# All batches' attention weights and values multiplied as float32, without splitting, in an attention and two-layer MoE kernel

## The chip, the cores and the metric

The kernel runs on one core of a Trainium2 chip. Its time is the device time of one execution in microseconds (us). TensorE multiplies matrices, VectorE, ScalarE and GpSimd work elementwise, and SyncE issues most of the transfers. In rows of the profile they are PE (PEld for its weight loads), DVE, ACT, POOL and SP.

## The reference

```
q, k, v: 8 batches x 8 heads x 576 x 64, float32
k_p, v_p = k, v averaged over groups of 8 positions      # 72 pooled positions
attn = softmax(q @ k_p.T / 8)                            # 576 x 72 per head
x = (attn @ v_p) as 4608 tokens x 512
h = max(x @ w1, x @ w2, x @ w3)                          # 4608 x 768
x = h @ w_out                                            # 4608 x 512
h = max(x @ w_in, 0);  out = (h * h) @ moe2_w_out        # 512 -> 2048 -> 512
```

## The kernel before

The 4608 tokens are worked on in 12 blocks of 384 for attention and the first layer, and then in 9 blocks of 512 for the second layer. A batch has 576 tokens, so it falls on the blocks in two pieces, one of 384 tokens and one of 192. A piece is worked on by pairs of heads, four pairs to a batch (`attend`): `load` brings k, q and v; `prepare` pools k into `kbd`; `softmax` multiplies (L353, into `sc`), takes the exponentials and normalises them; `transpose` turns the weights round on TensorE (L381, into `tr`) and copies them to `pt`; `values` multiplies them with the pooled values and writes `x`.

The products of the MoE layers are made exact to nearly float32 by splitting: a number is rounded to the reduced float32 type of TensorE (`fp32r` in rows), and what is lost becomes a second number of that type, so that the product is a sum of three reduced products (`PARTS`). `split` writes both halves: the high one by ScalarE (L133), the low one by VectorE or, for weights, GpSimd (L134).

Attention has two ways of forming the values, chosen by `whole = b < NATURAL`, where NATURAL is 1:

- Batch 0 (`whole`): its values are pooled by TensorE (`pool_v`). `transpose` copies the weights of one head by ScalarE (L389) and of the other by VectorE (L387), as float32. `values` makes one float32 product for each head, both into the one bank `av0` (L398), and splits the sum into `x`.
- Batches 1 to 7: VectorE pools the values (L242), and ScalarE and VectorE split them (L209, L210) into `vst`. The weights of each head are split on the way out of `tr` (L384, L385). `values` makes two reduced products for each head (L409 for the high half of the weights, L410 for the low), with the high and low values side by side in the stationary matrix, so that the two sums land in two halves of the partitions of bank `av0` or `av1`. ScalarE copies one half (L412), VectorE adds the other (L413), both through the buffer `xf`, and `xf` is split into `x`.

The transposed weights of the second head use bank `av1` too. Pieces of work are put into a list `todo` with due times and run in that order, after which a scheduler places each engine's instructions by its own timeline. In the first 115 us the weights of the first layer are converted as well (`convert`: L160 and L161 on ScalarE, L162 and L165 on VectorE; then L133 and L134 on GpSimd), on loads that share four `raw` buffers with k and v. Attention is woven into the first layer's products (L513, and L532 for its output) up to about 698 us; the second layer (L673, L797) runs from 762 us.

Of the kernel before, what the change touches and what calls it, by code (L numbers as in the profile page):

```python
# [10 lines left out]
F32 = mybir.dt.float32  # L11
F32R = mybir.dt.float32r
I32 = mybir.dt.int32
U32 = mybir.dt.uint32
AF = mybir.ActivationFunctionType
ALU = mybir.AluOpType
# [4 lines left out]
P = 128  # L21
B, H, S, D = 8, 8, 576, 64
POOL = 8
SP = S // POOL
NPAIR = H // 2
# [8 lines left out]
T1 = 384  # L34
# [35 lines left out]
NATURAL = 1  # L70
# [12 lines left out]
def as_f32(ap):  # L83
    return ap.bitcast(F32)
# [8 lines left out]
def attention_moe_kernel(ctx: ExitStack, tc: tile.TileContext, q, k, v, vn, w1, w2, w3, wo1, wi2, wo2, out):  # L93
    nc = tc.nc
# [12 lines left out]
    for sign, base in ((1, POOL * MID), (-1, POOL - 1 - POOL * MID)):  # L107
        nc.gpsimd.affine_select(
            out=sums, in_=sums, compare_op=ALU.is_ge, fill=0.0, base=base,
# [26 lines left out]
    def split(hl, src, engine=nc.vector):  # L136

        split_to(hl[:, 0], hl[:, 1], src, engine)
# [43 lines left out]
    t_p = s1.enter_context(tc.tile_pool(name="t_p", bufs=2))  # L182

    s_at = ctx.enter_context(ExitStack())
    kv_p = s_at.enter_context(tc.tile_pool(name="kv_p", bufs=1, side="right"))
    raw_p = s_at.enter_context(tc.tile_pool(name="raw_p", bufs=4, side="right"))
    sm_p = s_at.enter_context(tc.tile_pool(name="sm_p", bufs=4, side="right"))
    pt_p = s_at.enter_context(tc.tile_pool(name="pt_p", bufs=2, side="right"))
    xf_p = s_at.enter_context(tc.tile_pool(name="xf_p", bufs=1, side="right"))
    ah_p = s_at.enter_context(tc.tile_pool(name="ah_p", bufs=AHEAD, side="right"))  # L190
    sc_ps = s_at.enter_context(tc.tile_pool(name="sc_ps", bufs=2, space=PSUM))
    tr_ps = s_at.enter_context(tc.tile_pool(name="tr_ps", bufs=1, space=PSUM))
    av_ps = s_at.enter_context(tc.tile_pool(name="av_ps", bufs=1, space=PSUM))


    vst = kv_p.tile([SP, NPAIR, 4, D], F32R, name="vst")

    kbd = kv_p.tile([P, NPAIR, 2, SP], F32, name="kbd")
    nc.gpsimd.memset(kbd, 0.0)
    vst_f = []  # L200
    for _ in range(2):
        vf = t_p.tile([P, T1], F32, tag="ys", name="vst_f")[:SP].rearrange("s (p a d) -> s p a d", a=3, d=D)
        nc.gpsimd.memset(vf, 0.0)
        vst_f.append(vf)
    K_SCALE = 1.0 / (POOL * D**0.5)
    V_SCALE = 1.0 / POOL

    def split_scaled(hi, lo, src, scale):
        nc.scalar.activation(hi, src, AF.Copy, scale=scale)  # L209
        nc.vector.scalar_tensor_tensor(  # L210
            out=lo, in0=src, scalar=scale, in1=as_f32(hi), op0=ALU.mult, op1=ALU.subtract
        )


    spare = [f"spare{i}" for i in range(KF1)]
# [24 lines left out]
    def prepare_v(p, vr):  # L240
        vs = sm_p.tile([SP, 2, D], F32, tag="vs", name="vs", bufs=2)
        nc.vector.tensor_reduce(out=vs, in_=vr, axis=AX.X, op=ALU.add)  # L242
        split_scaled(vst[:, p, 0:4:3], vst[:, p, 1:3], vs, V_SCALE)

    def load_natural(b):

# [11 lines left out]
    def pool_v(tiles):  # L258
        vp = mm_ps.tile([P, 512], F32, tag="ps", name="vp")[:SP]
        last = (S - 1) // P  # L260
        for i in range(last + 1):
            n = min(P, S - i * P)
            c = MID - i * P // POOL
            nc.tensor.matmul(
                vp, lhsT=sums[:n, c : c + SP], rhs=tiles[i // 2][:n, i % 2], start=(i == 0), stop=(i == last)
            )
        for h in range(2):
            vh = vp.rearrange("s (p h d) -> s h p d", h=2, d=D)[:, h]
            for i in range(2):
                nc.scalar.activation(vst_f[i][:, :, 2 * h], vh[:, 2 * i : 2 * i + 2], AF.Copy, scale=V_SCALE)  # L270

    x_t = {}

# [45 lines left out]
    def attend(j, b, s0, n, p, t):  # L319

        kr, vr, qr, pt, sms = [], [], [], [], []
        first, whole = s0 == 0, b < NATURAL

        def load():
            if j == 0:
                kq = early([P, 2 * 512], "kq")
                kr.append(kq[:, :S])
                qr.append(kq[:, S : S + n])
                nc.sync.dma_start(out=kr[0], in_=k[b, p])
            elif first:  # L330
                kr.append(load_k(b, p))
            if j:
                qr.append(raw_p.tile([P, T1], F32, tag="qr", name="qr", bufs=4)[:, :n])
            nc.sync.dma_start(out=qr[0], in_=q[b, p, :, s0 : s0 + n])
            if first and b >= NATURAL:
                vr.append(load_v(b, p))

        def prepare():
            if first:
                prepare_k(p, kr[0])  # L340

        tiles = score_tiles(n)
        m = tiles[0][1]

        def softmax():
            if vr:
                prepare_v(p, vr.pop())
            g = len(tiles)
            sc = sc_ps.tile([P, 3 * 2 * SP], F32, tag="sc", name="sc")
            ss = scores(g)[:m]  # L350
            src = sc[:, : g * 2 * SP].rearrange("p (g h s) -> p g h s", h=2, s=SP)[:m]
            for i, (c, _) in enumerate(tiles):
                nc.tensor.matmul(src[:, i], lhsT=qr[0][:, c : c + m], rhs=kbd[:, p], start=True, stop=True)  # L353
            st = sm_p.tile([P, 3, 3, 2], F32, tag="st", name="st")[:m, :, :g]
            nc.vector.tensor_reduce(out=st[:, 0], in_=src, axis=AX.X, op=ALU.max, negate=True)  # L355
            for i in range(g):
                for h in range(2):
                    nc.scalar.activation(  # L358
                        ss[:, i, h], src[:, i, h], AF.Exp, bias=st[:, 0, i, h : h + 1],
                        accum_out=st[:, 1, i, h : h + 1],  # L360
                    )
            nc.vector.tensor_scalar_add(st[:, 1], st[:, 1], 1e-9)
            nc.vector.reciprocal(st[:, 2], st[:, 1])  # L363
            nc.gpsimd.tensor_tensor(  # L364
                out=ss, in0=ss,
                in1=st[:, 2].rearrange("p g (h o) -> p g h o", o=1).to_broadcast([m, g, 2, SP]), op=ALU.mult,
            )
            sms.append(ss)

        def transpose():  # L370
            if whole:
                pt.append(pt_p.tile([SP, 2, T1], F32, tag="pt", name="pt"))
            else:
                pt.append(pt_p.tile([SP, 2, 2, T1], F32R, tag="pt", name="pt"))
            for h in range(2):
                if h:
                    tr = av_ps.tile([P, T1], F32, tag="av1", name="tr")[:SP, :n]
                else:
                    tr = tr_ps.tile([SP, T1], F32, tag="tr", name="tr")[:, :n]
                for i, (c, _) in enumerate(tiles):  # L380
                    nc.tensor.transpose(tr[:, c : c + m], sms[0][:, i, h], ident[:m, :m])  # L381
                if not whole:
                    hi, lo = pt[0][:, 0, h, :n], pt[0][:, 1, h, :n]
                    nc.scalar.activation(hi, tr, AF.Copy)  # L384
                    nc.vector.tensor_tensor(out=lo, in0=tr, in1=as_f32(hi), op=ALU.subtract)  # L385
                elif h:
                    nc.vector.tensor_copy(pt[0][:, h, :n], tr)  # L387
                else:
                    nc.scalar.activation(pt[0][:, h, :n], tr, AF.Copy)  # L389

        def values():
            if t == 0:
                x_t[j][p] = x_p.tile([P, 2, T1], F32R, tag="x", name="x")
            x = x_t[j][p][:, :, t : t + n]
            if whole:
                av = av_ps.tile([P, T1], F32, tag="av0", name="av0")[:, :n]
                for h in range(2):
                    nc.tensor.matmul(  # L398
                        av, lhsT=vst_f[p // 2][:, p % 2, h : h + 2].rearrange("p a d -> p (a d)"), rhs=pt[0][:, h, :n],
                        start=(h == 0), stop=(h == 1),  # L400
                    )
                split(x, av)
                return
            hi, lo = pt[0][:, 0, :, :n], pt[0][:, 1, :, :n]
            xf = xf_p.tile([P, T1], F32, tag="xf", name="xf")[:, :n]
            for h in range(2):
                av = av_ps.tile([P, T1], F32, tag=f"av{h}", name=f"av{h}")[:, :n]
                lhsT = vst[:, p, 2 * h : 2 * h + 2].rearrange("p a d -> p (a d)")
                nc.tensor.matmul(av, lhsT=lhsT, rhs=hi[:, h], start=True, stop=False)  # L409
                nc.tensor.matmul(av, lhsT=lhsT, rhs=lo[:, h], start=False, stop=True)  # L410
                r, o = slice(h * D, (h + 1) * D), slice((1 - h) * D, (2 - h) * D)
                nc.scalar.activation(xf[r], av[o], AF.Copy)  # L412
                nc.vector.tensor_tensor(out=xf[r], in0=av[r], in1=xf[r], op=ALU.add)  # L413
            split(x, xf)

        return load, prepare, softmax, transpose, values

    w1_t, wo1_t = {}, {}
# [454 lines left out]
```

## Time and profile before

| | |
|---|---|
| median of three runs | 1467.43 us (1466.56 to 1469.72) |
| the profiled execution | 1465.84 us |
| its span, first to last instruction | 1464.0 us |
| TensorE busy | 1432.9 us (98%) |
| VectorE busy | 984.6 us (67%) |
| ScalarE busy | 763.9 us (52%) |
| GpSimd busy | 182.2 us (12%) |
| mean granted clock of TensorE | 0.993 |

The span leaves 1.8 us of the profiled execution's time outside. The busy time of an engine is the time in which at least one of its instructions is in flight; TensorE's instructions overlap, so that the distance between the starts of two of them, not their duration, says how long each holds up the next. A float32 product appears as two records of TensorE, a reduced product or a transpose as one.

### The profile page before, as it was taken

The page shows a single profiled execution, that of the slowest core. Times are in us where ns is not written, and L with a number is a line of the kernel's source. Part 1 is how long each engine was busy: PE and PEld are TensorE (multiplying, and loading weights), DVE is VectorE, ACT ScalarE, POOL GpSimd, SP SyncE. Part 2 cuts the span into 40 slices and gives each one's busy share as a digit, 9 for nine tenths or more (in the row PEclk, how much of TensorE's full clock was granted, in tenths as well). Part 3 has the DMA queues.
Part 4 walks back from the last instruction along what each step waited for, and adds up shares of the span by engine and source line. Part 5 has one row for each costly group of instructions (what it writes and reads, how often), then busy time and mean ns, then how long its engine had stood idle before and what let it go on. Part 6 is the DMA issues. An engine that isn't in the chain of part 4 may idle for free.

```text
span 1464.0 us, 27554 instructions
## 1 busy us (share of the span) xinstructions
PE 1432.9 (98%) x10410; PEld 1409.8 (96%) x10410; DVE 984.6 (67%) x1778; ACT 763.9 (52%) x1983; POOL 182.2 (12%) x228
## 2 busy tenths in 40 slices
PE   6989999999999999999999999999999999999998
PEld 4879999999999999999999999999999999999998
DVE  5896466766765856656426768687776768686765
ACT  7794366655665646655314535353444445454443
POOL 3451012222222212222000000000000000000000
PEclk9899999999999999999999999999999999999999
DMA  7553135443355434422539856666666666565746
GB/s 225 185 168 110 53 115 173 141 134 123 120 164 176 126 124 130 130 101 79 187 116 370 290 196 212 220 210 224 229 231 225 227 216 214 198 245 174 274 144 229
DMA packets 118307, 263.94 MB, mean 180 GB/s; under 512 B 12672, under 2 KB 62848, under 8 KB 118176
## 3 DMA queue, kind: packets, MB, share of 16 engines
q1 hardware_dynamic: 111264, 252.75, 51.0%
q10 hardware_dynamic: 6912, 9.44, 1.8%
q8 instruction: 82, 1.34, 0.4%
q14 instruction: 49, 0.40, 0.1%
HBM read 213.91 MB, written 48.23 MB: 179 GB/s over the span
## 4 chain that ended last, share of the span: by engine, by line
PE 88%; DMA 5%; ACT 3%; DVE 2%; issue 1%; POOL 0%; SPq 0%; DVEq 0%; ACTq 0%; POOLq 0%
PE ps L513 28%; PE ps L673 23%; PE ps L532 10%; PE accB L797 6%; PE accA L797 6%; DMA wo2s<-wo_dram 4%; PE accF L797 3%; PE accE L797 3%; PE sc L353 2%; PE accD L797 2%; PE tr L381 2%; PE av L410 1%; PE av L409 1%; ACT ss L358 1%; DVE wbits L165 1%
## 5 line engine op out<-in xcount | busy, mean ns | idle before, releaser
L513 PE MATMUL ps<-x,w 128*128 128x384 f32 x2592 | 495.7, 342 | 3.3 <-ACT w L133 1.2
L513 PEld LDWEIGHTS ps<-x,w 128*128 128x128 f32 x2592 | 452.0, 190 | 6.1 <-ACT w L133 2.6
L673 PE MATMUL ps<-y,wi2s 128*128 128x256 f32 x3024 | 371.8, 277 | 0.5 <-DVE c L644 0.2
L673 PEld LDWEIGHTS ps<-y,wi2s 128*128 128x128 f32 x3024 | 356.6, 188 | 1.9 <-DVE c L644 0.8
L532 PE MATMUL ps<-h,wo 128*128 128x384 f32 x864 | 162.1, 339 | 3.2 <-POOL wo L134 2.4
L532 PEld LDWEIGHTS ps<-h,wo 128*128 128x128 f32 x864 | 149.5, 189 | 4.0 <-POOL wo L134 2.8
L686 ACT ACTIVATE c<-c 128x512 f32<-128x512 f32 x90 | 56.3, 627 | 167.2 <-DVE c L644 166.6
L644 DVE TENSOR_TENSOR c<-ps,c 128x512 f32<-128x512 f32 x144 | 98.2, 687 | 66.0 <-PE ps L673 64.5
L521 DVE TENSOR_TENSOR hm<-ps,hm 128x384 f32<-128x384 f32 x144 | 79.5, 552 | 72.3 <-PE ps L513 69.9
L133 ACT ACTIVATE g<-c 128x512 fp32r<-128x512 f32 x144 | 90.2, 626 | 56.7 <-DVE c L683 23.3
L797 PE MATMUL accA<-wo2s,g 128*128 128x256 f32 x864 | 115.8, 277 | 0.0
L797 PE MATMUL accB<-wo2s,g 128*128 128x256 f32 x864 | 110.9, 277 | 2.6 <-DMA wo2s<-wo_dram 1.9
L134 DVE TENSOR_TENSOR g<-c,g 128x512 fp32r<-128x512 f32 x144 | 97.6, 685 | 16.2 <-ACT g L133 16.2
L797 PEld LDWEIGHTS accA<-wo2s,g 128*128 128x128 f32 x864 | 107.1, 188 | 0.0
L358 ACT ACTIVATE ss<-sc,st 128x72 f32<-128x72 f32 (+1 forms) x320 | 97.9, 319 | 17.6 <-DVE st L355 15.4
L797 PEld LDWEIGHTS accB<-wo2s,g 128*128 128x128 f32 x864 | 103.9, 188 | 3.2 <-ACT o L766 1.6
L364 POOL TENSOR_TENSOR ss<-ss,st 128x432 f32<-128x432 f32 (+1 forms) x64 | 56.4, 882 | 265.7 <-DVE st L363 182.9
L413 DVE TENSOR_TENSOR xf<-av,xf 64x192 f32<-64x192 f32 (+1 forms) x112 | 50.7, 453 | 46.7 <-ACT xf L412 44.8
L385 DVE TENSOR_TENSOR pt<-tr,pt 72x192 fp32r<-72x192 f32 (+1 forms) x112 | 49.3, 449 | 41.4 <-ACT pt L384 40.1
L412 ACT ACTIVATE xf<-av 64x192 f32<-64x192 f32 (+1 forms) x112 | 45.4, 405 | 54.5 <-PE av L410 40.4
L133 ACT ACTIVATE h<-hm 128x384 fp32r<-128x384 f32 x72 | 37.7, 523 | 64.2 <-DVE hm L521 63.9
L358 ACT ACTIVATION_READ_ACCUMULATOR ss<-sc,st 128x1 f32 (+1 forms) x320 | 65.8, 206 | 0.0
(104 smaller groups left out, 1951.4 us busy)
## 6 DMA issues: line engine op xcount, KB each, us to landing
wo2s<-wo_dram SPq DMA_DIRECT2D x252, 512.0 KB, 5.7
wi2s<-wi_dram SPq DMA_DIRECT2D x24, 512.0 KB, 9.1
wraw<-in_wo_dram SPq DMA_DIRECT2D x22, 512.0 KB, 3.7
wraw<-in_w_dram SPq DMA_DIRECT2D x18, 512.0 KB, 3.4
y_dram<-ys ACTq DMA_DIRECT2D x48, 192.0 KB, 2.0
wraw<-in_wi_dram SPq DMA_DIRECT2D x16, 512.0 KB, 3.5
wi_dram<-wraw SPq DMA_DIRECT2D x16, 512.0 KB, 3.7
wo_dram<-wraw SPq DMA_DIRECT2D x64, 128.0 KB, 2.0
```

The source lines that it names most:

```text
L133: nc.scalar.activation(hi, src, AF.Copy)
L134: engine.tensor_tensor(out=lo, in0=src, in1=as_f32(hi), op=ALU.subtract)
L358: nc.scalar.activation(ss[:, i, h], src[:, i, h], AF.Exp, bias=st[:, 0, i, h : h + 1], accum_out=st[:, 1, i, h : h + 1],)
L364: nc.gpsimd.tensor_tensor(out=ss, in0=ss, in1=st[:, 2].rearrange("p g (h o) -> p g h o", o=1).to_broadcast([m, g, 2, SP]), op=ALU.mult,)
L413: nc.vector.tensor_tensor(out=xf[r], in0=av[r], in1=xf[r], op=ALU.add)
L513: nc.tensor.matmul(ps, lhsT=w1_t[f, e][:, a, kk * P : (kk + 1) * P], rhs=x[kk][:, c], start=(n == 0), stop=(n == 3 * KD - 1),)
L521: nc.vector.tensor_tensor(out=hm, in0=ps, in1=hm, op=ALU.max)
L532: nc.tensor.matmul(ps, lhsT=wo1_t[kk][:, a, d * P : (d + 1) * P], rhs=hs[kk][:, c], start=(n == 0), stop=(n == 3 * KF1 - 1),)
L644: nc.vector.tensor_tensor(out=out, in0=in0, in1=in1, op=ALU.add)
L673: nc.tensor.matmul(bank[:, u * HT : (u + 1) * HT], lhsT=wi2_t[2 * gr + u][i][:, a, o + kk * P : o + (kk + 1) * P], rhs=y_t[j][m][:, c, kk] ...
L686: nc.scalar.activation(c, c, AF.Relu)
L797: nc.tensor.matmul(bank[:, i * 256 : (i + 1) * 256], lhsT=g[:, a, u * HT + i * P : u * HT + (i + 1) * P], rhs=w[:, u, c], start=(n == 0 an ...
```

## The change

Every batch is now handled as batch 0 was in `transpose` and `values`: the weights are copied once for each head, there is one float32 product for each head, and `x` is split straight from the bank. The branch for split values, the buffer `xf`, and `split_scaled` are gone; `vst` holds unsplit float32 values with a zero block between the heads, for all batches (batch 0's had buffers of their own). VectorE still pools the values of batches 1 to 7 (`prepare_v`), and ScalarE alone writes them to `vst`.

```diff
-    xf_p = s_at.enter_context(tc.tile_pool(name="xf_p", bufs=1, side="right"))
-    vst = kv_p.tile([SP, NPAIR, 4, D], F32R, name="vst")
-    vst_f = []
-    for _ in range(2):
-        vf = t_p.tile([P, T1], F32, tag="ys", name="vst_f")[:SP].rearrange("s (p a d) -> s p a d", a=3, d=D)
-        nc.gpsimd.memset(vf, 0.0)
-        vst_f.append(vf)
+    vst = kv_p.tile([SP, NPAIR, 3, D], F32, name="vst")
+    nc.gpsimd.memset(vst, 0.0)
...
-        split_scaled(vst[:, p, 0:4:3], vst[:, p, 1:3], vs, V_SCALE)
+        nc.scalar.activation(vst[:, p, 0:3:2], vs, AF.Copy, scale=V_SCALE)
...
-                if not whole:
-                    hi, lo = pt[0][:, 0, h, :n], pt[0][:, 1, h, :n]
-                    nc.scalar.activation(hi, tr, AF.Copy)
-                    nc.vector.tensor_tensor(out=lo, in0=tr, in1=as_f32(hi), op=ALU.subtract)
-                elif h:
+                if h:
                     nc.vector.tensor_copy(pt[0][:, h, :n], tr)
                 else:
                     nc.scalar.activation(pt[0][:, h, :n], tr, AF.Copy)
...
-            hi, lo = pt[0][:, 0, :, :n], pt[0][:, 1, :, :n]
-            xf = xf_p.tile([P, T1], F32, tag="xf", name="xf")[:, :n]
+            av = av_ps.tile([P, T1], F32, tag="av0", name="av0")[:, :n]
             for h in range(2):
-                av = av_ps.tile([P, T1], F32, tag=f"av{h}", name=f"av{h}")[:, :n]
-                lhsT = vst[:, p, 2 * h : 2 * h + 2].rearrange("p a d -> p (a d)")
-                nc.tensor.matmul(av, lhsT=lhsT, rhs=hi[:, h], start=True, stop=False)
-                nc.tensor.matmul(av, lhsT=lhsT, rhs=lo[:, h], start=False, stop=True)
-                r, o = slice(h * D, (h + 1) * D), slice((1 - h) * D, (2 - h) * D)
-                nc.scalar.activation(xf[r], av[o], AF.Copy)
-                nc.vector.tensor_tensor(out=xf[r], in0=av[r], in1=xf[r], op=ALU.add)
-            split(x, xf)
+                nc.tensor.matmul(
+                    av, lhsT=vst[:, p, h : h + 2].rearrange("p a d -> p (a d)"), rhs=pt[0][:, h, :n],
+                    start=(h == 0), stop=(h == 1),
+                )
+            split(x, av)
```

On TensorE, in the last block with attention, the last two pairs of batch 7 stood like this before (the number behind `av` is the buffer's, and the rows are in program order):

```order
L409 MATMUL av_7819<-pt,vst 128x384
L410 MATMUL av_7819<-pt,vst 128x384
L513 MATMUL ps<-x,w_4_0_643 128x384 x10
L513 MATMUL ps<-x,w_4_1_663 128x384 x12
L513 MATMUL ps<-x,w_4_2_717 128x384 x12
L513 MATMUL ps<-x,w_5_0_751 128x384 x12
L513 MATMUL ps<-x,w_5_1_805 128x384 x12
L409 MATMUL av_7935<-pt,vst 128x384
L410 MATMUL av_7935<-pt,vst 128x384
L409 MATMUL av_7940<-pt,vst 128x384
L410 MATMUL av_7940<-pt,vst 128x384
L513 MATMUL ps<-x,w_5_2_846 128x384 x12
```

And this is the same place after the change, where a row of a float32 product counts it once:

```order
L480 MATMUL ps<-x,w_3_1_579 128x384 x8
L365 MATMUL tr<-ident,ss 72x128 x6
L480 MATMUL ps<-x,w_3_1_579 128x384 x4
L377 MATMUL av_7233<-pt,vst 128x384 x2
L480 MATMUL ps<-x,w_3_2_599 128x384 x12
L480 MATMUL ps<-x,w_4_0_634 128x384 x12
L480 MATMUL ps<-x,w_4_1_654 128x384 x12
L480 MATMUL ps<-x,w_4_2_705 128x384 x12
L480 MATMUL ps<-x,w_5_0_739 128x384 x12
L480 MATMUL ps<-x,w_5_1_790 128x384 x12
L377 MATMUL av_7346<-pt,vst 128x384 x2
L480 MATMUL ps<-x,w_5_2_823 128x384 x12
```

For each pair, four reduced products (two buffers) became two float32 products into one buffer, which stand together between the first layer's products.

On VectorE, at the start, where the values of batch 1 are pooled (`vs<-vr`) while batch 0 is still worked on (`x<-av` ends a pair of it; `av_371` and `av_486` are its third and fourth pair of 384 tokens), the fourth reduction stood here before:

```order
L165 SCALAR_TENSOR_TENSOR wbits<-wraw,wbits 128x512
L134 TENSOR_TENSOR x<-av_371,x 128x384
L355 TENSOR_REDUCE st<-sc 96x4
L387 COPY pt<-tr 72x192
L355 TENSOR_REDUCE st<-sc 96x4
L363 RECIPROCAL st<-st 96x4
L210 SCALAR_TENSOR_TENSOR vst<-vs,vst 72x128
L162 SCALAR_TENSOR_TENSOR wbits<-wbits,wraw 128x512
L242 TENSOR_REDUCE vs<-vr 72x128
L165 SCALAR_TENSOR_TENSOR wbits<-wraw,wbits 128x512
L362 TENSOR_SCALAR st<-st 96x4
L134 TENSOR_TENSOR x<-av_486,x 128x384
```

After the change the third and the fourth reduction stand here (`av_594` is batch 0's second pair of 192 tokens, and `x<-av_536`, its first, is the row ahead of these):

```order
L350 RECIPROCAL st<-st 96x4
L230 TENSOR_REDUCE vs<-vr 72x128
L342 TENSOR_REDUCE st<-sc 96x4
L162 SCALAR_TENSOR_TENSOR wbits<-wbits,wraw 128x512
L367 COPY pt<-tr 72x192
L488 TENSOR_TENSOR hm<-ps,hm 128x384
L165 SCALAR_TENSOR_TENSOR wbits<-wraw,wbits 128x512
L349 TENSOR_SCALAR st<-st 96x4
L488 TENSOR_TENSOR hm<-ps,hm 128x384
L134 TENSOR_TENSOR x<-av_594,x 128x192
L350 RECIPROCAL st<-st 96x4
L230 TENSOR_REDUCE vs<-vr 72x128
```

Two of the four reductions have moved from ahead of batch 0's last pairs of 384 tokens to behind its first pairs of 192, since `vst` is now the buffer from which batch 0's products read too.

## Rows read from the trace of the kernel before

**Rows 1.** The page: span, and busy time of the engines.

```profile
span 1464.0 us, 27554 instructions
PE 1432.9 (98%) x10410; PEld 1409.8 (96%) x10410; DVE 984.6 (67%) x1778; ACT 763.9 (52%) x1983; POOL 182.2 (12%) x228
```

**Rows 2.** Stretches: length, busy us (instructions) of each engine, clock, DMA share, GB/s.

```profile
50.00:65.00 15.00, 14.94 (x96) 14.35 (x95) 14.44 (x32) 13.40 (x47) 8.06 (x9) 1.00 0.62 195
65.00:115.00 50.00, 42.69 (x236) 39.43 (x235) 47.42 (x81) 41.83 (x123) 26.57 (x19) 0.93 0.51 160
115.00:165.00 50.00, 50.00 (x300) 49.70 (x299) 28.54 (x54) 22.19 (x77) 4.99 (x6) 1.00 0.25 75
165.00:698.00 533.00, 532.51 (x3250) 528.37 (x3249) 339.38 (x718) 314.83 (x1015) 123.15 (x169) 1.00 0.40 129
```

**Rows 3.** The chain that ended last, one piece: start us, us, what.

```profile
328.19 7.65 PE ps L513 x44
```

**Rows 4.** Timeline of TensorE, reduced products of 384: start us, us, instruction, count.

```profile
304.14 0.34 PE L409 MATMUL av<-pt,vst 72*128 72x384 f32 x1
304.31 0.34 PE L410 MATMUL av<-pt,vst 72*128 72x384 f32 x1
304.49 0.90 PE L353 MATMUL sc<-kbd,qr 128*128 128x144 f32 x6
305.22 0.49 PE L381 MATMUL tr<-ident,ss 128*72 128x128 f32 x3
305.48 1.14 PE L513 MATMUL ps<-x,w 128*128 128x384 f32 x5
306.46 0.34 PE L409 MATMUL av<-pt,vst 72*128 72x384 f32 x1
```

**Rows 5.** Timeline of TensorE, reduced products of 192.

```profile
70.47 0.25 PE L409 MATMUL av<-pt,vst 72*128 72x192 f32 x1
70.56 0.27 PE L410 MATMUL av<-pt,vst 72*128 72x192 f32 x1
70.67 0.43 PE L353 MATMUL sc<-kbd,qr 128*128 128x144 f32 x2
```

**Rows 6.** Timeline of TensorE to 17.0 us, and then the whole group at 16.95.

```profile
15.56 0.82 PE L381 MATMUL tr<-ident,ss 128*72 128x128 f32 x6
16.21 0.90 PE L353 MATMUL sc<-kbd,kq 128*128 128x144 f32 x6
16.95 0.49 PE L398 MATMUL av<-pt,vst_f 72*128 72x384 f32 x1
...
16.95 1.46 PE L398 MATMUL av<-pt,vst_f 72*128 72x384 f32 x4
```

**Rows 7.** Timeline of TensorE, float32 products of 192.

```profile
64.10 0.82 PE L398 MATMUL av<-pt,vst_f 72*128 72x192 f32 x4
64.75 0.49 PE L381 MATMUL tr<-ident,ss 96*72 96x96 f32 x4
```

**Rows 8.** Groups of TensorE between 165 and 698 us, shapes apart: busy, mean | idle before.

```profile
L409 PE MATMUL av<-pt,vst 72*128 72x384 f32 x48 | 17.6, 366 | 0.0
...
L409 PE MATMUL av<-pt,vst 72*128 72x192 f32 x48 | 12.8, 266 | 0.0
```

**Rows 9.** Groups of VectorE in the whole span, shapes apart.

```profile
L387 DVE COPY pt<-tr 72x384 f32<-72x384 f32 x4 | 2.2, 549 | 0.0
...
L242 DVE TENSOR_REDUCE vs<-vr 72x128 f32<-72x1024 f32 x28 | 33.9, 1211 | 4.6 <-DMA vr<-in_v_dram 4.3
```

**Rows 10.** VectorE's L385 and then L413, in the stretch of 65 to 115.

```profile
65.00:115.00 50.00, 3.72 (x9) 0.93 0.51 160
...
65.00:115.00 50.00, 3.15 (x9) 0.93 0.51 160
```

**Rows 11.** Timeline of TensorE, 65 to 115 us: two of the waits (brackets: idle, releaser).

```profile
76.92 0.36 PE L409 MATMUL av<-pt,vst 72*128 72x192 f32 x1 [0.85 <-DVE xf L413]
...
111.25 0.69 PE L532 MATMUL ps<-h,wo 128*128 128x384 f32 x1 [2.44 <-POOL wo L134]
```

More of the change, by code (lines that the diff above doesn't have):

```diff
@@ L193, in attention_moe_kernel @@
     av_ps = s_at.enter_context(tc.tile_pool(name="av_ps", bufs=1, space=PSUM))
-    vst = kv_p.tile([SP, NPAIR, 4, D], F32R, name="vst")
     kbd = kv_p.tile([P, NPAIR, 2, SP], F32, name="kbd")
     nc.gpsimd.memset(kbd, 0.0)
-    vst_f = []
-    for _ in range(2):
-        vf = t_p.tile([P, T1], F32, tag="ys", name="vst_f")[:SP].rearrange("s (p a d) -> s p a d", a=3, d=D)
-        nc.gpsimd.memset(vf, 0.0)
-        vst_f.append(vf)
+    vst = kv_p.tile([SP, NPAIR, 3, D], F32, name="vst")
+    nc.gpsimd.memset(vst, 0.0)
     K_SCALE = 1.0 / (POOL * D**0.5)
     V_SCALE = 1.0 / POOL
[L208 to L212, printed above, removed]
     spare = [f"spare{i}" for i in range(KF1)]
@@ L268, in pool_v @@
             vh = vp.rearrange("s (p h d) -> s h p d", h=2, d=D)[:, h]
-            for i in range(2):
-                nc.scalar.activation(vst_f[i][:, :, 2 * h], vh[:, 2 * i : 2 * i + 2], AF.Copy, scale=V_SCALE)
+            nc.scalar.activation(vst[:, :, 2 * h], vh, AF.Copy, scale=V_SCALE)
     x_t = {}
@@ L321, in attend @@
         kr, vr, qr, pt, sms = [], [], [], [], []
-        first, whole = s0 == 0, b < NATURAL
+        first = s0 == 0
         def load():
@@ L370, in transpose @@
         def transpose():
[L371 to L374, printed above, removed]
+            pt.append(pt_p.tile([SP, 2, T1], F32, tag="pt", name="pt"))
             for h in range(2):
@@ L394, in values @@
             x = x_t[j][p][:, :, t : t + n]
[L395 to L403, printed above, removed]
-            hi, lo = pt[0][:, 0, :, :n], pt[0][:, 1, :, :n]
-            xf = xf_p.tile([P, T1], F32, tag="xf", name="xf")[:, :n]
-            for h in range(2):
-                av = av_ps.tile([P, T1], F32, tag=f"av{h}", name=f"av{h}")[:, :n]
-                lhsT = vst[:, p, 2 * h : 2 * h + 2].rearrange("p a d -> p (a d)")
-                nc.tensor.matmul(av, lhsT=lhsT, rhs=hi[:, h], start=True, stop=False)
-                nc.tensor.matmul(av, lhsT=lhsT, rhs=lo[:, h], start=False, stop=True)
-                r, o = slice(h * D, (h + 1) * D), slice((1 - h) * D, (2 - h) * D)
-                nc.scalar.activation(xf[r], av[o], AF.Copy)
-                nc.vector.tensor_tensor(out=xf[r], in0=av[r], in1=xf[r], op=ALU.add)
-            split(x, xf)
+            av = av_ps.tile([P, T1], F32, tag="av0", name="av0")[:, :n]
+            for h in range(2):
+                nc.tensor.matmul(
[3 more added lines that the diff above has]
+            split(x, av)
         return load, prepare, softmax, transpose, values
```

## The prediction

> **What bounds the kernel now.** I read the page first. There TensorE is busy for 1432.9 us of the 1464.0 us span, VectorE for 984.6 and ScalarE for 763.9 [rows 1]. The reader is to see that TensorE is the likely bound, but a busy share is an average, so the table of stretches comes next [rows 2]. From 115 to 165 us and from 165 to 698 us, TensorE is busy without a gap (50.00 of 50 us, 532.51 of 533) at a granted clock of 1.00, which is its level of 2.4 GHz, while VectorE works for 339.38 us of the 533 and ScalarE for 314.83. Most of the attention lies here.
>
> The stretch from 65 to 115 us is another matter: TensorE is busy for 42.69 us of 50, its clock is 0.93 on the mean, and VectorE works for 47.42. There the conversion of weights sets the pace.
>
> A busy TensorE may still be slow, since a record lasts 0.34 us and overlaps with the next. So I looked at the distances of the starts. In the chain of work that ended last, 44 records of L513 take 7.65 us, 0.174 each [rows 3]. At 304 us a short piece of attention stands between such products [rows 4]: two value products, six score records and three transposes, and then five of L513, from 304.14 to 306.46. At the distances that each kind has elsewhere (0.175, 0.123 from the six at 16.21, 0.108 from the six at 15.56 [rows 6], and 0.174) they should take 2 x 0.175 + 6 x 0.123 + 3 x 0.108 + 5 x 0.174 = 2.28 us, and they take 2.32. The array is fed as fast as it takes its work. So whatever the change adds to TensorE's work in these stretches moves the end, and what it takes from VectorE and ScalarE there does not.
>
> **The change part by part.**
>
> *TensorE's products.* Before, a head of a piece took two reduced products. For 384 tokens they start 0.17 to 0.18 us apart (304.14, 304.31, 304.49 [rows 4]), so I take 0.175 each. For 192 tokens the distances are 0.09 and 0.11 [rows 5], 0.10 each. Now a head takes one float32 product, which is two records. Batch 0 shows its price: four records of 384 tokens take 1.46 us in all, the last of them 0.49 in flight, so three distances take 0.97 us, 0.323 each [rows 6]. Four records of 192 tokens reach from 64.10 to 64.75, 0.1625 each [rows 7]. The number of records stays the same, two for each head, and each holds the array 1.6 to 1.9 times as long.
>
> A pair of heads therefore costs 4 x (0.323 - 0.175) = 0.59 us more for 384 tokens and 4 x (0.1625 - 0.10) = 0.25 us more for 192. From 165 to 698 us there are 48 heads of each width [rows 8], 24 pairs of each: 24 x 0.59 + 24 x 0.25 = 20.2 us. The other 4 + 4 pairs of the 28 + 28 lie between 65 and 165 us: 4 x 0.59 + 4 x 0.25 = 3.4 us. Some 2.1 of it (seven heads of 384) is in the full stretch up to 165 us, and 1.3 in the stretch with gaps. The new products also end more often next to reduced ones. Such a step loses time: the piece at 304 us, which holds one, took 0.04 us over its sum. The program has 158 such steps now, after 142, which adds 16 x 0.04 = 0.6 us.
>
> The Trainium skill speaks of this price in two ways. "FP8 and Floating Point Precision", section TensorE Precision Notes, has true float32 as four passes through the array; "Perfetto Trace Analysis", section Engine Utilization, halves the array's output rate for FP32_LOW_HIGH. By the first the sum would rise by nearly what the rows give; by the second one float32 product would cost what two reduced ones do, and the array's work would stay as it is. The distances of batch 0's records agree with the first, and the second is a rival below.
>
> *VectorE and ScalarE.* For each head, L384, L385, L412 and L413 go, and for each pair one copy on either engine comes (L387 on VectorE takes 549 ns for 384 tokens [rows 9]). L210 goes too. In the full stretches this lies beside TensorE's products, which hide it before and after, so I cost it at nothing there. If that cover were gone, TensorE would be waiting for its operands, which the rows do not show: L409 has 0.0 us idle ahead of it from 165 us on [rows 8].
>
> *The start.* Between 65 and 115 us, L385 and L413 are 9 + 9 instructions of 3.72 + 3.15 = 6.9 us [rows 10]. Four or five copies come for them, most of 192 tokens; at up to 0.55 us each they are some 2 us. Against that, two reductions of batch 1's values, 1.2 us each [rows 9], stood ahead of batch 0's last pairs before 50 us and now wait until batch 0's products have read `vst`; they fall into the stretch from 50 to 65 us or later, where VectorE already works for 14.44 us of 15 [rows 2]. Queued behind them on VectorE are the conversions L162 and L165, for which GpSimd's low halves and so L513 wait; a raw buffer stays taken until its reduction is done, and SyncE's next load into it waits. Net, VectorE is relieved of about 6.9 - 2 - 2.4 = 2.5 us by 115 us. TensorE idles for 7.3 us there (50 - 42.69), some of it for L413 (0.85 at 76.92) and the longest, 2.44, for GpSimd's `wo` [rows 11]. What the start gives back is not to be read from one row, so I bound it. At best all 7.3 us of idle time and 0.07 x 50 = 3.5 us of the lower clock come back, 10.8 us. At worst the two late reductions and what waits behind them cost their own 2.4 us, and the loads behind the taken raw buffers as much again, near 5 us more. I take what VectorE is relieved of, 2.5 us back, since it is the fullest engine there.
>
> *The rest.* The clearing of `vst` is one instruction of GpSimd for two, hidden by the first loads. The second layer's transfers and products stand in the same order as before, and I count nothing there.
>
> Sum: 20.2 + 2.1 + 1.3 + 0.6 - 2.5 = 21.7 us. Added to the profiled execution's own 1465.84 us this gives 1487.5 us. That execution was 1.6 us under the median of the runs (1467.43) and 0.7 under the fastest of them (1466.56), which is little beside the rest, so I leave it at that: about 1.4% slower.
>
> **The rivals.**
>
> *The start gains all it can.* With the 7.3 us of idle time and the 3.5 us of clock back, the sum is 24.2 - 10.8 = 13.4 us, 1479 us. For it: VectorE is busy for 47.42 us of 50 there, and it is relieved. Against it: the longest wait, 2.44 us, is for GpSimd's `wo`, whose work does not change, and TensorE gets more to do.
>
> *The start loses.* Batch 1's values come late through the shared `vst`, the two reductions and the loads behind their raw buffers hold back the weights: 24.2 + 5 = 29 us, 1495 us. For it: VectorE is full at 50 to 65 us. Against it: the array takes longer over its attention there too, which gives the conversions time.
>
> *Not slower: the products of batch 0 are dear for another reason.* If a float32 product at full rate cost only as much as two reduced ones, and batch 0's distances came from its unsettled surroundings, TensorE's work would stay and the start alone would count: 1465.84 - 2.5 = 1463 us, within 0.2%; with all of the start back, 1455 us. This decides if records of 384 tokens start 0.175 us apart in the full stretch. Against it: the distances of 0.1625 us at 64.10 fall amid products at full clock, directly between other records, with no wait. The Trainium skill's "Perfetto Trace Analysis", section Engine Utilization, would have it so; the distance at 64.10 does not agree with it.
>
> **How the numbers follow.** The start as forecast, within a few us: 0.70. The start gains all: 0.12. The start loses: 0.13. Not slower: 0.05, of which I give 0.02 to faster and 0.03 to the same. A change of 0.2% is about what a measurement of this kernel can tell from none, 3 us; every other case lies 12 us or more above the time before, so slower has 0.95. The range runs from the one case of the start to just short of the other, 1479 to 1494 us.
>
> **What would show it.** Right: in the stretch after 165 us, records of the new product line start 0.32 and 0.16 us apart, TensorE has no gaps, and the stretch of attention after 165 us grows by about 21 us; VectorE's busy time falls clearly under 984.6 us and the time does not follow; the second layer is shifted and no longer or shorter than before. Wrong: distances of 0.175 us; gaps of TensorE ahead of the value products or the transposes; or a start that ends more than 6 us away from where it ended before.

## The result, and the profile after

The changed kernel takes 1487.52 us, the median of 4 runs (1486.05 to 1488.27), against 1466.99 us for the kernel before, also of 4 runs (1466.37 to 1469.72). The ratio is 1.0135 with an interval of 1.0117 to 1.0153, so the kernel is some 17 to 22 us slower. The profiled execution took 1488.27 us, 1484.1 of them its span. I forecast 1487.5 us. The total is right; this section and the next show which terms of the sum are.

The page of the changed kernel begins with the same rows as [rows 1]; the last row here is the group of the new value products, from part 5 of the page.

```profile
span 1484.1 us, 27230 instructions
PE 1451.3 (98%) x10410; PEld 1414.6 (95%) x10410; DVE 902.4 (61%) x1582; ACT 699.2 (47%) x1813; POOL 177.0 (12%) x227
...
L377 PE MATMUL av<-pt,vst 72*128 72x384 f32 (+1 forms) x256 | 75.1, 413 | 2.8 <-DVE x L134 2.8
```

TensorE has as many instructions as before (10410) and is busy for 18.4 us longer (1451.3 - 1432.9). VectorE is busy for 82 us less and ScalarE for 65 us less, and the time does not follow them. That is the case in one line: work went away on two engines that the array hardly waited for, and the array, which sets the time, got dearer work in the same number of instructions.

The table of stretches, with the columns of [rows 2], in the changed kernel:

```profile
65.00:115.00 50.00, 46.08 (x267) 42.05 (x266) 44.61 (x71) 40.40 (x121) 31.89 (x21) 1.00 0.51 160
115.00:165.00 50.00, 49.92 (x288) 48.42 (x287) 20.67 (x34) 13.76 (x47) 1.08 (x2) 1.00 0.26 83
165.00:712.00 547.00, 547.00 (x3233) 531.80 (x3233) 269.37 (x556) 261.21 (x885) 117.59 (x171) 1.00 0.40 128
```

TensorE is again without a gap after 165 us, at a granted clock of 1.00, while VectorE falls from 339.38 us of 533 to 269.37 of 547. Between 65 and 115 us TensorE is busier than before (46.08 us against 42.69).

The price of the new products stands in the timeline of TensorE in that full stretch (start, us, instruction, count):

```profile
227.48 0.81 PE L377 MATMUL av<-pt,vst 72*128 72x192 f32 x4
...
324.58 0.42 PE L480 MATMUL ps<-x,w 128*128 128x384 f32 x1
324.84 1.45 PE L377 MATMUL av<-pt,vst 72*128 72x384 f32 x4
325.83 0.98 PE L480 MATMUL ps<-x,w 128*128 128x384 f32 x3
```

L377 is the value product, L480 the first layer's input product (L513 before). How long one record is in flight stands in the groups of TensorE from 165 to 712 us, shapes apart (busy, mean ns of one | idle before):

```profile
L377 PE MATMUL av<-pt,vst 72*128 72x384 f32 x96 | 35.2, 485 | 0.0
L377 PE MATMUL av<-pt,vst 72*128 72x192 f32 x96 | 19.7, 325 | 0.0
```

At 227.48 three distances take 0.81 - 0.325 = 0.485 us, 0.162 each. At 324.84 they take 1.45 - 0.485 = 0.965 us, 0.322 each. These are batch 0's prices of [rows 6, 7] (0.323 and 0.1625), now amid an undisturbed stretch.

**Laying the stretches side by side.** Windows at the same clock times hold different work in the two kernels. So I marked the same point of the program in every trace: the start of the 433rd of the first layer's 2592 input products, with which its third block begins, and the start of the last one. One row for each kernel, with the columns of [rows 2]. The kernel before:

```profile
177.37:745.60 568.23, 567.74 (x3453) 563.66 (x3451) 354.95 (x746) 324.10 (x1032) 126.43 (x172) 1.00 0.40 131
```

The changed kernel:

```profile
174.06:759.62 585.56, 585.56 (x3457) 570.68 (x3455) 287.15 (x586) 271.43 (x901) 119.96 (x173) 1.00 0.39 127
```

The reader is to see 585.56 - 568.23 = 17.3 us in this stretch, which holds the 24 + 24 pairs of the prediction's main term (all but one head's product of 384, which here falls ahead of it, while six score records that fell ahead of it before now lie in it; the two cancel to 0.1 us), and again no idle time of TensorE. To see how far such differences can be trusted I profiled both kernels twice more. This table is worked out from the starts of the records in each trace (us; the last column is from the second layer's first product to its last):

```
kernel                 433rd at   433rd to last   second layer
before                  177.4        568.2          701.7
before, second          175.7        568.2          707.2
before, third           174.8        568.3          704.9
changed                 174.1        585.5          707.6
changed, second         181.1        585.5          708.6
changed, third          175.2        585.5          703.8
```

The middle stretch repeats to 0.1 us. Between executions of the same kernel the start differs by up to 7.0 us, and the second layer, whose instructions the change leaves as they are, by up to 5.5. So the 17.3 us are firm, the second layer shows no effect of the change that stands out from its scatter (its 701.7 in the first profile was the shortest of all), and the start can't be judged from one profile.

### The profile page after: what moved, and what is told of

Read it like the earlier page. It is cut to its first block, busy times and chain, and to the rows that moved or that the text cites. A ratio compares the mean times of both kernels' runs of the same rounds, so it can differ in the third digit from the quotient of the medians.

```text
span 1484.1 us, 27230 instructions
## 1 busy us (share of the span) xinstructions
PE 1451.3 (98%) x10410; PEld 1414.6 (95%) x10410; DVE 902.4 (61%) x1582; ACT 699.2 (47%) x1813; POOL 177.0 (12%) x227
## 4 chain that ended last, share of the span: by engine, by line
PE 85%; DMA 9%; DVE 3%; ACT 2%; issue 1%; SPq 0%; DVEq 0%; ACTq 0%
PE ps L480 27%; PE ps L640 22%; PE ps L499 9%; PE accA L764 6%; PE accB L764 6%; DMA wo2s<-wo_dram 4%; PE av L377 3%; PE accE L764 3%; PE accF L764 3%; PE sc L340 2%; PE tr L365 2%; PE accD L764 1%; DMA vr<-in_v_dram 1%; DMA wraw<-in_w_dram 1%; DMA yr<-y_dram 1%
## 5 line engine op out<-in xcount | busy, mean ns | idle before, releaser
L480 PE MATMUL ps<-x,w 128*128 128x384 f32 x2592 | 494.2, 343 | 2.6 <-POOL w L134 1.1
L480 PEld LDWEIGHTS ps<-x,w 128*128 128x128 f32 x2592 | 450.4, 189 | 11.2 <-POOL w L134 1.6
L351 POOL TENSOR_TENSOR ss<-ss,st 128x432 f32<-128x432 f32 (+1 forms) x64 | 53.4, 834 | 256.9 <-DVE st L350 186.2
L377 PE MATMUL av<-pt,vst 72*128 72x384 f32 (+1 forms) x256 | 75.1, 413 | 2.8 <-DVE x L134 2.8
L134 DVE TENSOR_TENSOR h<-hm,h 128x384 fp32r<-128x384 f32 x72 | 48.8, 677 | 38.1 <-ACT h L133 38.1
L486 ACT ACTIVATE hm<-ps 128x384 f32<-128x384 f32 x72 | 35.3, 490 | 60.8 <-PE ps L480 59.4
```

Of the source, the lines that this page charges most:

```text
L134: engine.tensor_tensor(out=lo, in0=src, in1=as_f32(hi), op=ALU.subtract)
L351: nc.gpsimd.tensor_tensor(out=ss, in0=ss, in1=st[:, 2].rearrange("p g (h o) -> p g h o", o=1).to_broadcast([m, g, 2, SP]), op=ALU.mult,)
L377: nc.tensor.matmul(av, lhsT=vst[:, p, h : h + 2].rearrange("p a d -> p (a d)"), rhs=pt[0][:, h, :n], start=(h == 0), stop=(h == 1),)
L480: nc.tensor.matmul(ps, lhsT=w1_t[f, e][:, a, kk * P : (kk + 1) * P], rhs=x[kk][:, c], start=(n == 0), stop=(n == 3 * KD - 1),)
```

## The experiments

**The relief without the price.** For batches 1 to 7 this kernel takes everything from the change but the float32 product: each head has two reduced products of the same shapes. For that `pt` is of the reduced type as well as `vst` (not shown).

```diff
-    vst = kv_p.tile([SP, NPAIR, 3, D], F32, name="vst")
+    vst = kv_p.tile([SP, NPAIR, 3, D], F32R, name="vst")
...
+                if b < NATURAL:
+                    nc.tensor.matmul(av, lhsT=as_f32(vals), rhs=as_f32(weights_), start=(h == 0), stop=(h == 1))
+                    continue
+                for k in range(2):
+                    nc.tensor.matmul(
+                        av, lhsT=vals, rhs=weights_, start=(h == 0 and k == 0), stop=(h == 1 and k == 1)
+                    )
```

Expected: 

> The changed kernel, in which batches 1 to 7 form their values with two reduced products for each head in place of one float32 product, over the same operands, so that TensorE has as many records as before and as after, only shorter ones (this leaves out the low halves and makes the values twice as large). Theory: the 20 us are the array's time over the longer records, and the relief of VectorE and ScalarE counts only at the start. Then the 17 to 21 us of the stretch after 165 us go and the gain of the start stays: 1461 to 1466 us. Rival: the order of the new products, their one bank or the waits around them cost the time; then it stays above 1475 us.

Measured: 1463.87 us (9 runs) against 1469.08 (20 runs), ratio 0.9967 (0.9952 to 0.9981): 4.8 us faster than before (2.8 to 7.1). The same stretch of its trace:

```profile
172.20:738.65 566.45, 566.45 (x3452) 564.23 (x3451) 286.57 (x583) 268.25 (x888) 119.56 (x172) 1.00 0.41 131
```

VectorE and ScalarE work as little here as in the changed kernel, and TensorE is as full; the stretch takes 566.45 us against 585.56. Those 19.1 us are the price of the float32 products: nothing else differs but the places of a few pieces among the products. The rival that a float32 product costs no more than two reduced ones falls. Against the kernel before, the stretch is 1.8 us shorter, although VectorE has 68 us less to do in it: that is the most that the relief is worth there. The other 3 us of the 4.8 lie outside this stretch, and the start, at 172.2 us here, is where the work changed. The median lies in the middle of the 1461 to 1466 us expected.

**The price twice.** The changed kernel with each value product issued twice.

```diff
-                nc.tensor.matmul(
-                    av, lhsT=vst[:, p, h : h + 2].rearrange("p a d -> p (a d)"), rhs=pt[0][:, h, :n],
-                    start=(h == 0), stop=(h == 1),
-                )
+                for k in range(2):
+                    nc.tensor.matmul(
+                        av, lhsT=vst[:, p, h : h + 2].rearrange("p a d -> p (a d)"), rhs=pt[0][:, h, :n],
+                        start=(h == 0 and k == 0), stop=(h == 1 and k == 1),
+                    )
```

Expected: 

> The changed kernel, in which every float32 value product is made twice into the same bank (so the values are twice as large). Theory: each record is on the path with its 0.323 or 0.1625 us, so the 32 + 32 pairs of all batches cost 32 x 4 x 0.323 + 32 x 4 x 0.1625 = 62 us more: 1549 us, and in the stretch from product 432 of the first layer to its last, 24 + 24 pairs cost 46.5 us, 632 us. Rival: some of it lies in waits, and the time grows by clearly less, under 40 us.

Measured: 1549.55 us (4 runs), ratio to the kernel before 1.054 (1.0509 to 1.0571). The stretch:

```profile
191.50:824.60 633.10, 633.10 (x3648) 605.48 (x3647) 289.33 (x586) 272.93 (x901) 119.41 (x173) 1.00 0.37 118
```

It grew by 47.5 us with 192 more records. At 0.323 and 0.1625 us for 96 records of each width they should take 46.6. Every added record is on the path at its full price, and there is no slack into which a dearer product could go. The expected 1549 us for the whole came out too.

**The changed kernel once more, beside the doubled products.** Expected: 

> The changed kernel a third time, timed and profiled. Theory: the stretch from product 432 to the last of the first layer takes 585.5 us as in its two other profiles, while the start (174.1 and 181.1 us to product 432) and the second layer (707.6 and 708.6 us) scatter; the median lies within 3 us of 1.35% above that of before. Rival: the start's 174.1 us is the rule and 181.1 a single disturbance; then it is within 1 us of 174.1.

Measured: 1489.1 us (5 runs), ratio 1.0133 (1.011 to 1.0157), which repeats the result. The stretch took 585.5 us again, and the start and the second layer (175.2 and 703.8 us) lie between or below the earlier ones. That is scatter, but 175.2 is only 1.1 us from 174.1, and none of the other kernels here with batch 1 on the new way and single value products starts the stretch later than 174.7, so a start near 174 may be the rule and 181.1 the exception.

**Batch 1 alone, and all but batch 1.** Batch 1's 4 + 4 pairs are those of the start. The kernel before, with the new products for batch 1 only (its condition is `b < 2`), and with them for every batch but 1 (`b != 1`; there GpSimd also clears a slice of `vst` for batch 2, and in the former all of `vst` at the start; neither is shown):

```diff
-        split_scaled(vst[:, p, 0:4:3], vst[:, p, 1:3], vs, V_SCALE)
+        if whole:
+            nc.scalar.activation(vst[:, p, 0:3:2], vs, AF.Copy, scale=V_SCALE)
+        else:
+            split_scaled(vst[:, p, 0:4:3], vst[:, p, 1:3], vs, V_SCALE)
...
-        first, whole = s0 == 0, b < NATURAL
+        first, whole = s0 == 0, b < 2
...
+                vals = vst_f[p // 2][:, p % 2] if b < NATURAL else as_f32(vst[:, p])
```

Expected of batch 1 alone: 

> The kernel before, in which batch 1 alone goes the new way as well (its values are kept as the high half alone, as its buffer is of the reduced type). Theory: the start gives back about 6.7 us against 3.4 us of longer products, as the two traces show, so it is some 3 us faster than before, 1463 to 1464 us. Rival: the earlier end of the start is chance or comes from the later batches; then it costs its 3.4 us, 1470 us.

Expected of all but batch 1: 

> The kernel before, in which batches 2 to 7 alone go the new way (their values are kept as the high half alone). Theory: the start is as before and the stretch after it is 17 us longer, as the two traces show: 1484 us if the second layer's 5.9 us more in the changed kernel's profile were chance, 1490 us if the change causes them. Rival: without the relief at the start the cost is the predicted 20 us and more.

Measured: batch 1 alone 1469.95 us (12 runs), ratio 1.0009 (0.9995 to 1.0022), so +1.3 us with an interval of -0.7 to 3.2. All but batch 1: 1487.51 us (6 runs), ratio 1.0116 (1.0094 to 1.0137), so +17.0 us with 13.8 to 20.1. The two add up to 18 us, beside 19.5 to 19.8 for the whole change. The slowdown lies in batches 2 to 7, as the steady stretch says, and batch 1 gives back about what it costs. For batch 1 alone the theory failed: I expected it 3 us faster from one pair of traces, and the interval leaves at most 0.7 us of that; the rival's 3.4 us of cost lies just outside it too. For the others the 17 us came as expected.

**Batch 0's values in their own buffers.** The changed kernel with `vst_f` as before, so that batch 1's reductions do not wait for batch 0's products (that `pool_v` writes there is not shown).

```diff
+    vst_f = []
+    for _ in range(2):
+        vf = t_p.tile([P, T1], F32, tag="ys", name="vst_f")[:SP].rearrange("s (p a d) -> s p a d", a=3, d=D)
+        nc.gpsimd.memset(vf, 0.0)
+        vst_f.append(vf)
...
+            vals = vst_f[p // 2][:, p % 2] if b < NATURAL else vst[:, p]
```

Expected: 

> The changed kernel, in which batch 0's pooled values have buffers of their own again, so that batch 1's reductions need not wait for batch 0's products. Theory of the prediction: the two reductions that moved cost VectorE 2.4 us where it is full, so the block of first-layer products that ends the start is reached up to 2.4 us earlier: 1485 us. Rival: they are hidden, and the time stays within 1 us of the changed kernel's 1487.5.

Measured: 1486.55 us (6 runs), ratio 1.0114 (1.0095 to 1.0134), which overlaps with the changed kernel's 1.0135 (1.0117 to 1.0153). The 433rd product starts at 174.7 us, in the changed kernel at 174.1 to 181.1. By the ratios this kernel is some 3 us faster than the changed one, with an uncertainty of about 4 us, so neither the theory's 2.4 us nor the rival's nothing is ruled out: what the late reductions cost stays open.

**Single profiles, to see the scatter.** Expected of the kernel before: 

> The kernel before once more, for its profile. The second layer, whose instructions are the same in all these kernels, took 701.7 us in the profile of before and 702.4 to 707.6 in those of the five others. Theory: it varies from execution to execution, so here it lies anywhere from 701 to 708, and the first layer ends within 1 us of 758.1. Rival: the change lengthens it; then it is 701.7 again, within 1 us.

Of the same once more: 

> The kernel before a third time, for the same question: by the theory the second layer takes another length between 701 and 708 us, by the rival 701.7 once more.

Of the changed kernel: 

> The changed kernel once more, for its profile. Theory: product 432 of L480, the first of the third block, starts within 1 us of 174.1 (it was at 177.4 before), the first layer ends within 1 us of 772.1, and only the second layer's length moves. Rival: the start's gain is chance, and these times move by several us.

Of batch 1 alone: 

> The kernel in which batch 1 alone was added to the new way, once more, for its profile. Its first layer ended at 754.6 us, 3.5 before that of before, while its median was the same. Theory: the gain at the start is real and lies within 1 us of this again, and the second layer's scatter hid it in the medians. Rival: the first layer ends near 758.

Measured: 1469.86, 1466.62, 1493.93 and 1469.87 us, with one run of the kernel before on that chip at 1473.91. The first two and the third are in the table above; batch 1 alone has its 433rd product at 173.9 us and 569.0 us from there to the last. In all four the second layer scatters as the theory has it. The theories on the start did less well. The kernel before started the last product of its first layer at 756.4 and then 755.5 us, not within 1 us of 758.1. The changed kernel had its 433rd product at 181.1, not within 1 us of 174.1, as the rival had it. Batch 1 alone came to that product at 755.4, within 1 us of 754.6 as expected, but the third profile of before has it at 755.5, so this gain is not shown.

The changed kernel's 1493.93 is mostly its start: the wait of TensorE that comes last there stands in its timeline (in brackets the idle time and its releaser).

```profile
139.76 21.09 PE L480 MATMUL ps<-x,w 128*128 128x384 f32 x120 [1.88 <-DVE hm L488]
```

And the chain of waits that leads to it (start, us, what):

```profile
121.95 3.42 DMA vr<-in_v_dram
125.49 1.23 DVE vs L230
126.73 3.79 DMA vr<-in_v_dram
130.61 1.22 DVE vs L230
131.83 0.66 DVE ks L223
132.52 5.95 DMA kr<-in_k_dram
138.52 0.64 issue
139.16 0.56 DVE hm L488
```

The reductions of the values and the keys wait for their loads, `hm` stands behind them on VectorE, and TensorE waits for `hm`. This is the way in which the rival "the start loses" would go. It appeared in one of three profiles, and the changed kernel's first trace has no wait of TensorE between 130 us and the second layer. It is not the whole of the 7 us by which this start is longer: the waits of TensorE after 115 us come to 2.2 us here and to 0.1 in the first profile. The rest stands beside a lower granted clock (0.93 against 1.00 from 65 to 115 us), and no run takes the two apart.

## Why the prediction was right, step by step

**The bound.** Right. TensorE sets the time in the steady stretch: the doubled products lengthened it by 47.5 us where 46.6 were worked out, and 68 us less of VectorE's work shortened it by 1.8.

**The array's price: 20.2 us and 0.6 for the steps.** The unit prices of the float32 records are right to 0.001 us. The sum is a little too large: 20.8 predicted, 19.1 measured between two reduced products and one float32 one (17.3 net of the relief, where I had said that the stretch would grow by about 21). What failed is the step term. I took 0.04 us for a step from a float32 group to a reduced one from the single place at 304 us [rows 4], and let more steps mean more loss. Adding up each record's undisturbed distance (worked out from the traces: 0.174 for the products of 384, 0.122 for scores, 0.109 and 0.0825 for transposes of 128 and 96, and for values 0.322 and 0.162, or 0.175 and 0.101 reduced) leaves this for all steps and waits of the stretch:

```
kernel                 sum of distances   measured   left   steps
before                     564.3            568.2     3.9    108
two reduced products       564.3            566.5     2.2     77
changed                    584.4            585.5     1.2    122
```

Half a ns more or less on the 0.174 moves what is left by 1.4 us, but by the same in all three, so the comparison stands: the changed kernel has the most steps and loses least. Taken one by one in its trace, the 44 steps behind value products lose some 0.003 us each, and those behind scores and transposes of 128 no more; only the 21 behind transposes of 96 lose 0.03. At 304 us a transpose of 128 stood ahead of the step, and the 26 such steps of the kernel before lose 0.005 us on the mean, so the place that I read was not a typical one. The change brings steps that cost nearly nothing, and of those behind transposes of 96 it leaves 21 of 36 (as the kernel with two reduced products does): against the kernel before, the term is nearer -0.3 us than 0.6. Between the last two rows of the table it is 0.1, which leaves some 1.2 us of the difference between 20.8 and 19.1 that I did not take apart. The row at 324.84 shows a step behind value products of 384 tokens: four value products and then L480, whose third record starts at 325.83 + 0.98 - 0.34 = 326.47. From 324.84 that is 1.63 us, and 4 x 0.322 + 2 x 0.174 = 1.64: the step costs nothing. It only looks as if it did, since the first L480 is recorded early (325.83, one distance of 0.03 us after the last value product) and the second late.

**VectorE and ScalarE at nothing in the full stretch.** Nearly right: 1.8 us came back. Some of it is one wait of the kernel before that I had overlooked; the group of L409 that I read has none, but the products after it do. In the kernel before, the timeline of TensorE:

```profile
660.57 0.42 PE L409 MATMUL av<-pt,vst 72*128 72x384 f32 x1
660.83 0.34 PE L410 MATMUL av<-pt,vst 72*128 72x384 f32 x1
661.66 1.14 PE L513 MATMUL ps<-x,w 128*128 128x384 f32 x5 [0.49 <-ACT hm L519]
```

From 660.83 to 661.66 there are 0.83 us where a distance of 0.175 is due. TensorE waits for ScalarE's `hm` for 0.49 us of it. That wait is gone in the changed kernel and in the one with two reduced products, so some 0.65 of the 1.8 us is shown. Some 0.4 more lies in the steps behind transposes of 96 (36 against 21, at 0.03 us). The rest, 0.7 us, is spread over the first layer's own products, and its cause stays open.

**The start: 3.4 us more, 2.5 back.** The net of 0.9 us agrees with batch 1 alone (+1.3, -0.7 to 3.2). The relief of 4.8 us, less 1.8 in the steady stretch, leaves about 3 us for the start, near my 2.5, with an uncertainty of 2 us either way. TensorE's idle time between 65 and 115 us points the same way. The two further profiles of before, and then of the changed kernel, in the columns of [rows 2]:

```profile
65.00:115.00 50.00, 44.44 (x251) 40.19 (x250) 47.10 (x81) 42.37 (x125) 24.24 (x19) 0.97 0.52 162
65.00:115.00 50.00, 44.09 (x248) 41.28 (x247) 45.86 (x83) 42.80 (x124) 25.81 (x20) 0.93 0.53 159
...
65.00:115.00 50.00, 45.82 (x249) 42.47 (x248) 42.03 (x68) 38.93 (x117) 28.30 (x19) 0.93 0.49 155
65.00:115.00 50.00, 47.15 (x264) 42.87 (x262) 43.81 (x71) 40.34 (x118) 30.33 (x20) 0.97 0.52 161
```

With the first profile of each, TensorE is idle for 7.3, 5.6 and 5.9 us of the 50 before and for 3.9, 4.2 and 2.9 after, some 2.6 less on the mean. With batch 1 alone it is 3.6 and 4.4, with all but batch 1 5.6. So the relief of batch 1's work does give idle time back. The 3.4 us of longer products in the start were not measured by themselves. My bounds, from 10.8 us back to 5 us lost, were far wider than what came of it. I had read the clock of 0.93 between 65 and 115 us as something that the change might give back. In the changed kernel's three profiles it is 1.00, 0.93 and 0.97, in those of before 0.93, 0.97 and 0.93, so one profile's clock in the start belongs to that execution.

**The second layer at nothing.** Right, though by my own test (no longer or shorter than before) the pair of first profiles said otherwise: 701.7 against 707.6 us. The two further profiles of each kernel (704.9 and 707.2, 703.8 and 708.6) show that a difference of this size is scatter.

**The base.** The profiled execution of before, 1465.84 us, was a quick one: that kernel's medians beside these experiments were 1466.99 to 1469.08. The change costs 19.5 to 19.8 us by the ratios, where I summed 21.7 on a base that was 1 to 3 us low. They are of nearly the same size and opposite sign, so that the forecast met the median to 0.1 us is luck; that it lay within 2 to 3 us is not.

The one kernel here that is faster than the one before, by 0.33%, leaves part of the computation out; there is no other.

## What to carry to other kernels

Where one engine is full, price a change by the distances between the starts of that engine's records, and count what it saves elsewhere as next to nothing: here 82 us less on VectorE bought 5 us, and the same number of records on TensorE at 1.6 to 1.9 times the distance cost 19. Before reading a difference of a few us between two profiles, mark the same instruction in both and profile each kernel again; a stretch that repeats to 0.1 us can lie between two that scatter by 5 to 7. A loss per step read from a single place should not be multiplied by a count before the whole stretch has been added up.

## What the runs showed of the hardware

- A float32 product of 384 columns is two records of 0.322 us, 0.644 together, 3.7 times the 0.174 of a reduced one; for 192 columns it is two of 0.162 against one of some 0.10, 3.2 times. This holds in the full stretch at a granted clock of 1.00. The Trainium skill's "FP8 and Floating Point Precision", section TensorE Precision Notes, has true float32 as four passes through the array; the trace agrees in size.
- After a float32 group the first reduced product is recorded only 0.03 us behind the last float32 record, and its successor late by nearly what the first was early: behind value products of 384 columns the two distances are 0.028 and 0.471 us, 0.499 together, where 0.322 + 0.174 = 0.496 are due. Behind transposes of 96 columns the pair does lose 0.03 us. A distance read from one of the two misleads.
- The second layer's transfers and products are the same in both kernels and took 701.7 to 708.6 us. In the changed kernel's first trace TensorE waits there for `wo2s` transfers, 0.08 to 1.56 us at a time. The longest stands ahead of the same product near the end in all three profiles of this kernel, with 1.56, 2.99 and 1.38 us, and in the first of before with 1.48; of the shorter ones some come and go between executions and others change their length.
